# Pooled attention and a softplus feed-forward layer on one core: a chunk's steady attention regrouped into four interludes

## The chip, the cores and the metric

The program runs on one core of one Trainium2 chip. The metric is the device time of one execution in microseconds (us). TensorE (PE) multiplies matrices; its weight loads (PEld) run beside the multiplications. VectorE (DVE), ScalarE (ACT) and GpSimd (POOL) work on vectors, SyncE (SP) issues the transfers.

## The reference

```python
# q, k, v: (8, 8, 576, 64); pool = 8, Sp = 72
k_p = k.reshape(B, H, Sp, pool, D).mean(axis=3)
v_p = v.reshape(B, H, Sp, pool, D).mean(axis=3)
scores = scale * np.matmul(q, k_p.transpose(0, 1, 3, 2))
scores = scores - np.max(scores, axis=-1, keepdims=True)
attn = np.exp(scores)
attn = attn / (np.sum(attn, axis=-1, keepdims=True) + 1e-09)
attn_out = np.matmul(attn, v_p)
x = attn_out.transpose(0, 2, 1, 3).reshape(B * S, H * D)      # 4608 x 512
h = x @ w_in                                                  # 4608 x 2048
g = np.maximum(h, 0.0) + np.log1p(np.exp(-np.abs(h)))
return (g @ w_out).astype(np.float32)                         # 4608 x 512
```

## The kernel before

**Tiling.** The 4608 tokens are worked through in 18 chunks of 256 (`CT`), each of two tiles of 128 tokens. A chunk needs attention (its output x is 512 wide), then the first product (x with w_in), softplus, and the second product (with w_out). The feed-forward layer of a chunk runs in eight pairs u = 0 to 7, each of two blocks of 128 columns of w_in. Every number is kept as a rounded value and a rest, so that each product becomes three matmuls. In the steady part a pair is one block of 24 matmuls into `h` (line 562, 128x256 each, `pair1`) and one block of 21 matmuls into `m` (line 710, `pair2_fast`; seven products in place of eight). The blocks alternate on PE in a fixed order: h of pair u, then m of pair u - 1. After a block h, ACT makes g and its rounded part gh (lines 570, 584), DVE the sums `sf` (lines 621 to 624) and the rest gl (591), ACT rounds the sums (`so`, 635), DVE takes their rest (640); then the pair's block m may run.

**Attention one chunk ahead.** While chunk c runs through its eight pairs, the attention of chunk c + 1 is finished and that of c + 2 begun; its PE work stands as *interludes* between the blocks, sometimes inside a block h. Per tile these are: four transposes of q (`qT`, line 359), 32 small matmuls for the scores (`scores`, line 379, quarters of the array), four transposes of the normed probabilities (`PT`, 440) and two transposes of the probabilities of the last eight keys, in three copies (`last`, 452). Per chunk there is one interlude more, the values (`av_products`, 481 and 488). It has 20 matmuls, and 40 where the 256 tokens of the chunk belong to two batches of 576 tokens; below these are called split chunks (chunks 4, 6, 11, 13 and 15). In five chunks there are also four transposes of pooled keys (`kT`, line 232).

**Around them.** q goes from PSUM through ACT (366) to the scores; the scores through DVE (minimum 386, subtraction 393) into E; one exponential of ACT for both tiles (323, with a change of the activation table before and after it, placed behind the softplus of pair 2); then per tile DVE's sum (410), reciprocal (414, 415), `main` (419, keys 0 to 63) and `ends` (426, last eight keys), PE's transposes, ACT's copies (`PT_out` 447, `last_high` 459) and DVE's `last_low` (464); after the values ACT and DVE make x (495, 498).

**What sets the order.** `Order.run` (lines 52 to 100) is a list planner. Each `op(engine, cost, fn, after, slots, first)` has a planned cost, the operations it waits for, and slots (buffers of a kind) that it holds; the planner picks for each engine the operation with the longest remaining path plus `first` among those that could start by then or within `PAUSE` = 0.4 us. Each engine then executes its own list strictly in that order and waits where data are late. The kinds of slots (1259 to 1262) bound what may overlap: eight PSUM banks make two for the blocks h (`h`), four for accumulation (two of them kind `acc`), two for all of attention (`bank`); there are one `q`, one `pe`, two `qT`, one `E`, six `G`.

`steady_attention(c)` (1277) is called at pair 1 of chunk c - 1 and lists load, q and scores; `probabilities` (1309) lists the rest behind the exponential.

Of the kernel before, what the change touches and what calls it, by code (L numbers as in the profile page):

```python
# [30 lines left out]
class Order:  # L31
# [72 lines left out]
def pooled_attention_softplus_ffn(  # L104
# [9 lines left out]
    nc = tc.nc  # L114
# [220 lines left out]
    def load_q(c):  # L335
        new_q(c)
        for t in range(T):
            load_q_tile(c, t)
# [12 lines left out]
    class Tile:  # L351

        def __init__(self, c, t):
            self.c, self.t, self.first = c, t, c * CT + t * P
            self.ts = slice(t * P, (t + 1) * P)
# [106 lines left out]
        def last_low(self, ps):  # L462
            o = last_[self.c][R:2 * R, :, self.ts]
            nc.vector.tensor_tensor(
                out=o, in0=ps[R:2 * R, 0:2 * P].rearrange("p (a i) -> p a i", a=2),
                in1=o.bitcast(F32), op=ALU.subtract)

    def av_products(c, pss):

        pt, lt = pt_[c], last_[c]
        sp = [(b % 2, slice(lo - c * CT, hi - c * CT)) for lo, hi, b in spans(c * CT, (c + 1) * CT)]
        for g in range(2):
            for i, t in sp:
                for e in range(2):
                    for r, ps in enumerate(pss):
                        rows, n = slice(r * KM, (r + 1) * KM), 2 * g + e

                        nc.tensor.matmul(  # L481
                            out=ps[e * D:(e + 1) * D, g * CT + t.start:g * CT + t.stop],
                            lhsT=vs[i][rows, n], rhs=pt[rows, n, t],
                            start=g == 0 and t.start == 0, stop=False)
# [272 lines left out]
    def act(n):  # L757
        return 0.14 + 0.00094 * n
# [4 lines left out]
    def dve2(n):  # L763
        return 0.14 + 0.00106 * n
# [494 lines left out]
    kinds = {"h": other[:2], "acc": other[2:4], "bank": other[4:], "ld": LD, "q": "a", "pT": "a", "qT": Q, "lt_": "a",  # L1259
             "pe": "a", "mn": "ab", "sm": "ab", "E": "a", "kp": "a", "vp": "a", "S": "ab", "x": "b",  # L1260
             **{y.kind: {"a": "b", "b": "a"}[y.name] for y in last_g},
             "G": [f"G{i}" for i in range(4)] + O}
    ends = {e: max(o.end for o in todo.ops if o.engine == e) for e in (ACT, DVE, PE, SYNC)}
# [1 line left out]
    todo.begin = {e: max(0, t - ends[PE]) for e, t in ends.items()}  # L1265
    op = todo.op
    EXP, third = 2, {}
    HURRY, EARLY = 60, 100
    MM = 0.1195
    x_slot, x_done = {N1: taken[-1]}, {N1: []}  # L1270
    for x in (qT_done, score_done, av_done, k_ready, v_ready):
# [2 lines left out]

    parts_of = lambda n, k: [o for b in sorted({b for _, _, b in n}) for o in k.get(b, ())]

    def steady_attention(c):
        s_q, s_E, s_lt = Slot("q"), Slot("E"), Slot("lt_")
        tiles = [Tile(c, t) for t in range(T)]

        def load():
            load_q(c)
        o_q = op(SYNC, 3.0, load, qT_done.get(c - 1, ()), [s_q], lag=2.4)
        subs = []
        qT_done[c], score_done[c], av_done[c], x_done[c] = [], [], [], []
        for x in tiles:
            sp = spans(x.first, x.first + P)
            s, s_qT, s_mn = Slot("bank"), Slot("qT"), Slot("mn")
            o = op(PE, 0.45, lambda x=x, s=s: x.qT(bank(s, "qTp")), [o_q, *av_done.get(c - 1, ())],
                   [s_q, s], first=EARLY)  # L1290
            qT_done[c].append(o)
            o = op(ACT, act(512), lambda x=x, s=s, n=s_qT: x.qT_out(s.tile, n.name),
                   [o], [s, s_qT])
            last, ss = [], [Slot("bank"), Slot("bank")]
            p = op(PE, 0.7, lambda x=x, ss=ss: x.scores([bank(s, "sc") for s in ss]),
                   [o, *parts_of(sp, k_ready)], [s_qT, *ss], first=EARLY)
            score_done[c].append(p)
            for i, s in enumerate(ss):
                last = [op(DVE, 0.46, lambda x=x, i=i, s=s, n=s_mn: x.least(i, s.tile, n.name), [p, *last],
                           [s, s_mn])]  # L1300
# [5 lines left out]
                subs.append(op(DVE, 0.46, less, last, [s, s_mn, s_E]))  # L1306
        return lambda where: probabilities(c, tiles, s_E, s_lt, subs, where)

    def probabilities(c, tiles, s_E, s_lt, subs, where):

        s_pT, lows = Slot("pT"), []
        ex = op(ACT, 1.2 + TABLE, lambda: exponential(e_[c]), [*subs, where], [s_E])
        op(ACT, TABLE, lambda: None, [ex], first=5000)
        for x in tiles:
            s_sm, s_pm, s_pe = Slot("sm"), Slot("G"), Slot("pe")
            o = op(DVE, 0.76, lambda x=x, n=s_sm: x.sum(n.name), [ex], [s_E, s_sm])
            o = op(DVE, 0.38, x.reciprocal, [o], [s_sm])
            m = op(DVE, 0.7, lambda x=x, s=s_pm: x.main(s.name), [o], [s_E, s_sm, s_pm])
            e = op(DVE, 0.52, x.ends, [o], [s_E, s_sm, s_pe])
            s, r = Slot("bank"), Slot("bank")  # L1320
            o = op(PE, 0.45, lambda x=x, s=s: x.PT(bank(s, "ptp")), [m], [s, s_pm], first=EARLY)
            lows.append(op(ACT, act(512), lambda x=x, s=s: x.PT_out(s.tile), [o], [s, s_pT]))
            o = op(PE, 0.15, lambda x=x, r=r: x.last(bank(r, "ltp")), [e], [r, s_pe], first=EARLY)
            h = op(ACT, act(256), lambda x=x, r=r: x.last_high(r.tile), [o], [r, s_lt])
            lows.append(op(DVE, dve2(256), lambda x=x, r=r: x.last_low(r.tile), [h], [r, s_lt]))

        def values(after=()):
            sp = spans(c * CT, (c + 1) * CT)
            ss = [Slot("bank"), Slot("bank")]
            o = op(PE, 1.55 if len(sp) == 1 else 2.1,  # L1330
                   lambda: av_products(c, [bank(s, "avp") for s in ss]),
                   [*lows, *parts_of(sp, v_ready), *after], [*ss, s_lt, s_pT], first=EARLY)
            av_done[c].append(o)
            return o, ss
        o, ss = values()
        s_x = x_slot[c] = Slot("x")
        for r, s in enumerate(ss):
            o = op(ACT, act(512), lambda r=r, s=s: av_high(c, r, s.tile, s_x.name), [o], [s, s_x])
            x_done[c].append(op(DVE, dve2(512), lambda r=r, s=s: av_low(c, r, s.tile), [o], [s, s_x]))

    def first_products(c, u, before):
        fast = c >= NF
# [164 lines left out]
```

## Time and profile before

| what | value |
|---|---|
| median of 3 runs | 900.37 us (899.27 to 901.25) |
| span of the profiled execution | 899.4 us |
| PE busy in it | 884.2 us (98%) |
| PEld, DVE, ACT busy | 837.0, 649.1, 406.4 us |
| chain that ended last | 93% PE |
| read from and written to HBM | 167.25 and 22.54 MB |

Of the profiled execution the page gives the span, from the first instruction to the last; the runs are timed around the whole execution. The page's busy shares are averages over the span: up to about 187 us the weights are converted and the first three chunks are worked, up to 247 us chunk 3 runs with undivided second products, and from then to the end the steady pairs described above repeat.

In the rows below a line of the timeline merges neighbouring instructions of one kind: its first number is when the first of them started, the second how long they took together up to the modelled end of the last. Matmuls overlap, so what a block costs is read as the start of the next block less its own start.

### The profile page before, as it was taken

The page shows a single profiled execution, that of the slowest core. Times are in us where ns is not written, and L with a number is a line of the kernel's source. Part 1 is how long each engine was busy: PE and PEld are TensorE (multiplying, and loading weights), DVE is VectorE, ACT ScalarE, POOL GpSimd, SP SyncE. Part 2 cuts the span into 40 slices and gives each one's busy share as a digit, 9 for nine tenths or more (in the row PEclk, how much of TensorE's full clock was granted, in tenths as well). Part 3 has the DMA queues.
Part 4 walks back from the last instruction along what each step waited for, and adds up shares of the span by engine and source line. Part 5 has one row for each costly group of instructions (what it writes and reads, how often), then busy time and mean ns, then how long its engine had stood idle before and what let it go on. Part 6 is the DMA issues. An engine that isn't in the chain of part 4 may idle for free.

```text
span 899.4 us, 20521 instructions
## 1 busy us (share of the span) xinstructions
PE 884.2 (98%) x8308; PEld 837.0 (93%) x8308; DVE 649.1 (72%) x1601; ACT 406.4 (45%) x824; POOL 2.4 (0%) x19
## 2 busy tenths in 40 slices
PE   7999999999999999999999999999999999999997
PEld 3788989888999999999999999999999999999997
DVE  5989999888767778777667766777566565747454
ACT  5954343354353545444444435353545344434332
POOL 1000000000000000000000000000000000000000
PEclk9999999999999999999999999999999999999999
DMA  8974535455897777687658775677556565636472
GB/s 237 297 239 166 187 128 169 156 197 169 286 287 250 226 242 258 224 235 238 216 187 262 225 222 199 215 252 229 209 172 222 193 211 185 237 143 223 177 239 89
DMA packets 107085, 191.12 MB, mean 212 GB/s; under 512 B 46064, under 2 KB 60400, under 8 KB 106992
## 3 DMA queue, kind: packets, MB, share of 16 engines
q1 hardware_dynamic: 106992, 189.82, 64.9%
q8 instruction: 65, 1.06, 0.5%
q14 instruction: 28, 0.23, 0.1%
HBM read 167.25 MB, written 22.54 MB: 211 GB/s over the span
## 4 chain that ended last, share of the span: by engine, by line
PE 93%; DMA 3%; DVE 2%; SPq 1%; ACT 1%; issue 0%; DVEq 0%; ACTq 0%
PE h L562 37%; PE m L710 30%; PE acc L536 7%; PE h L514 7%; PE acc L603 3%; PE sc L379 2%; PE qTp L359 2%; PE avp L481 2%; PE ptp L440 1%; DMA wst<-in_moe_w_in_dram 1%; PE avp L488 1%; DMA w<-wi 1%; PE ltp L452 1%; DMA q<-in_q_dram 1%; DVE o L731 0%
## 5 line engine op out<-in xcount | busy, mean ns | idle before, releaser
L562 PE MATMUL h<-x,w 128*128 128x256 f32 x2880 | 354.4, 279 | 1.1 <-DVE x L498 0.8
L562 PEld LDWEIGHTS h<-x,w 128*128 128x128 f32 x2880 | 339.6, 188 | 2.6 <-PE acc L536 1.2
L570 ACT ACTIVATE g<-h 128x512 f32<-128x512 f32 x120 | 71.8, 598 | 277.6 <-PE h L562 277.5
L710 PE MATMUL m<-w,so 128*128 128x256 f32 x1344 | 172.4, 277 | 0.0
L710 PEld LDWEIGHTS m<-w,so 128*128 128x128 f32 x1344 | 162.3, 188 | 0.1
L710 PE MATMUL m<-w,gh 128*128 128x256 f32 x672 | 131.0, 284 | 0.0
L621 DVE TENSOR_TENSOR sf<-g 128x128 f32<-128x128 f32 x112 | 32.6, 291 | 134.2 <-ACT g L570 133.7
L710 PEld LDWEIGHTS m<-w,gh 128*128 128x128 f32 x672 | 101.6, 188 | 1.7
L635 ACT CAST so<-sf 128x512 fp32r<-128x512 f32 x112 | 69.7, 622 | 57.4 <-DVE sf L624 57.1
L640 DVE TENSOR_TENSOR so<-sf,so 128x512 fp32r<-128x512 f32 x112 | 77.3, 690 | 22.4 <-ACT so L635 22.4
L710 PE MATMUL m<-w,gl 128*128 128x256 f32 x336 | 93.4, 278 | 0.0
L514 PEld LDWEIGHTS h<-x,w 128*128 128x128 f32 x576 | 71.8, 188 | 3.3 <-DVE w L849 0.4
L514 PE MATMUL h<-x,w 128*128 128x256 f32 x576 | 73.3, 279 | 0.0
L591 DVE TENSOR_TENSOR gl<-g,gh 128x384 fp32r<-128x384 f32 (+1 forms) x120 | 67.3, 561 | 2.2 <-PE ltp L452 1.7
L710 PEld LDWEIGHTS m<-w,gl 128*128 128x128 f32 x336 | 63.1, 188 | 0.0
L519 ACT ACTIVATE g<-h 128x256 fp32r<-128x256 f32 x96 | 32.2, 383 | 65.9 <-PE h L514 46.5
L536 PE MATMUL acc<-w,g 128*128 128x512 f32 x192 | 61.0, 398 | 0.0
L584 ACT ACTIVATE gh<-h 128x384 fp32r<-128x384 f32 (+1 forms) x120 | 59.3, 494 | 0.0
L731 DVE TENSOR_TENSOR o<-o,m 128x256 f32<-128x256 f32 x98 | 39.7, 418 | 3.3 <-ACT o L723 0.4
L536 PE MATMUL acc<-w,gl 128*128 128x512 f32 x96 | 38.0, 396 | 1.0 <-DVE gl L525 1.0
L536 PEld LDWEIGHTS acc<-w,g 128*128 128x128 f32 x192 | 33.3, 188 | 5.4
L624 DVE TENSOR_TENSOR sf<-g,sf 128x128 f32<-128x128 f32 x112 | 32.7, 292 | 3.9
(170 smaller groups left out, 979.7 us busy)
## 6 DMA issues: line engine op xcount, KB each, us to landing
w<-wi SPq DMA_DIRECT2D x224, 512.0 KB
out_dram<-o SPq DMA_DIRECT2D x36, 256.0 KB
q<-in_q_dram SPq DMA_DIRECT2D x32, 256.0 KB
wst<-in_moe_w_in_dram SPq DMA_DIRECT2D x32, 256.0 KB
wst<-in_moe_w_out_dram SPq DMA_DIRECT2D x16, 512.0 KB
wi<-w SPq DMA_DIRECT2D x16, 512.0 KB
kst<-in_k_dram SPq DMA_DIRECT2D x24, 288.0 KB
vst<-in_v_dram SPq DMA_DIRECT2D x24, 256.0 KB
```

The lines of the kernel that those rows point to most:

```text
L514: nc.tensor.matmul(out=ps[:, 0:CT], lhsT=row(w, kc), rhs=x[:, kc], start=first and kc == j == 0, stop=last and kc == KC - 1 and j == 2)
L536: nc.tensor.matmul(out=accs[c][t], lhsT=a[:, ts], rhs=w, start=f == 0 and j == 0, stop=f == FC - 1 and j == 2)
L562: nc.tensor.matmul(out=ps[:, k * CT:(k + 1) * CT], lhsT=row(w, kc), rhs=x_[c][i][:, kc], start=first and n == 0, stop=last and n == len(or ...
L570: nc.scalar.activation(out=g, in_=x.rearrange("p (b i) -> p b i", i=P), func=AF.Softplus)
L584: nc.scalar.activation(out=gh, in_=quarters(c, x.rearrange("p (b i) -> p b i", i=P)), func=AF.Softplus)
L591: nc.vector.tensor_tensor(out=gl, in0=quarters(c, g), in1=gh.bitcast(F32), op=ALU.subtract)
L621: tt(out=sf[:, 2], in0=g[:, 0], in1=g[:, 2], op=ALU.add)
L624: tt(out=sf[:, 3], in0=g[:, 3], in1=sf[:, 1], op=ALU.subtract)
L635: nc.scalar.copy(out=so[:, 0], in_=ss[c, u])
L640: nc.vector.tensor_tensor(out=so[:, 1], in0=sf, in1=so[:, 0].bitcast(F32), op=ALU.subtract)
L710: nc.tensor.matmul(out=ms[c][n], lhsT=x, rhs=y, start=u == 0 and j == 0 and n in (1, 6, 5, 4), stop=u == FP - 1 and j == 2 and n in (2, 7, ...
L731: nc.vector.tensor_tensor(out=o, in0=in0, in1=m[n], op=how)
```

## The change

The steady part's attention (chunk 4 and later) is listed anew; what is computed stays the same.

- PE: the two tiles' `PT` and the four transposes of the last keys become one operation of 12 transposes, which waits for `main` of both tiles and for `ends`. The values and the first four q transposes of the *next* chunk become one operation, which also waits for the load of that q. The scores of tile 0 and the q transposes of tile 1 become one operation. The scores of tile 1 stay alone.
- Banks: the last keys (of both tiles together, in one bank), and both q transposes, use a bank of kind `h`; before they used kind `bank`.
- DVE: one sum, one addition and one reciprocal for both tiles; `ends` in three instructions for both tiles in place of four; `last_low` once in place of twice. ACT: `last_high` once in place of twice. `pe` (now for both tiles) takes a buffer of kind `qT`.
- SP: the load of the next chunk's q is listed with the probabilities, still behind the q transposes of the chunk before.
- Planner: minima, subtractions, `last_high` and `last_low` get `first=FRONT` (20).

```diff
-             "pe": "a", "mn": "ab", "sm": "ab", "E": "a", ...
+             "pe": "a", "mn": "ab", "sm": "a", "E": "a", ...
-    HURRY, EARLY = 60, 100
+    HURRY, EARLY, FRONT = 60, 100, 20
+    class Chunk:
...
+        def sum(self, tag):
+            sm = self.sm = small.tile([P, T * H], F32, tag="sm" + tag, name="sm")
+            nc.vector.tensor_reduce(out=sm, in_=self.E(), axis=AX.X, op=ALU.add)
...
+        def ends(self, tag):
+            self.pe = one.tile([P, 2 * T, 3, R], F32, tag=tag, name="pe")
+            for n in range(3):
+                nc.vector.tensor_tensor(out=self.pe[:, :, n]..., in0=self.E()[:, :, KM:SP]..., op=ALU.mult)
+        def PT(self, pss, psl):
+            for t, ps in enumerate(pss):
+                for n in range(HP):
+                    nc.tensor.transpose(out=ps[:, n * P:(n + 1) * P], in_=self.pm[t][:, 2 * n:2 * n + 2]..., identity=ident)
+            for t in range(T):
+                for a in range(2):
+                    nc.tensor.transpose(out=psl[0:3 * R, a * CT + t * P:...], in_=self.pe[:, 2 * t + a]..., identity=ident)
...
     def steady_attention(c):
+        if c not in firsts:
+            first_q(c)
...
+        for t, x in enumerate(tiles_[c]):
+            r = Slot("h") if t == 0 else None
+            def scores(t=t, x=x, ss=ss, r=r):
+                x.scores([bank(s, "sc") for s in ss])
+                if t == 0:
+                    tiles_[c][1].qT(bank(r, "qTp"))
+            p = op(PE, 1.15 if t == 0 else 0.7, scores, [o, *parts_of(..., k_ready)],
+                   [s_qT, *ss, *([r, s_q] if t == 0 else [])], first=EARLY)
...
+    def probabilities(c, s_E, s_lt, subs, where):
...
+        o = op(DVE, 1.65, lambda: x.sum(s_sm.name), [ex], [s_E, s_sm])
+        e = [op(DVE, 0.7, lambda t=t: x.main(t, s_pm[t].name), [o], [s_E, s_sm, s_pm[t]]) for t in range(T)]
+        e.append(op(DVE, 0.8, lambda: x.ends(s_pe.name), [o], [s_E, s_sm, s_pe]))
+        bs = [Slot("bank"), Slot("bank"), Slot("h")]
+        o = op(PE, 1.3, lambda: x.PT([bank(s, "ptp") for s in bs[:2]], bank(bs[2], "ltp")), e,
+               [*bs, *s_pm, s_pe], first=EARLY)
+        h = op(ACT, act(512), lambda: x.last_high(bs[2].tile), [o], [bs[2], s_lt], first=FRONT)
+        lows = [op(DVE, dve2(512), lambda: x.last_low(bs[2].tile), [h], [bs[2], s_lt], first=FRONT)]
+        lows += [op(ACT, act(512), lambda t=t: x.PT_out(t, bs[t].tile), [o], [bs[t], s_pT]) for t in range(T)]
...
+        if more:
+            load_queries(c + 1)
+            r, (s_q, o_q) = Slot("h"), q_loads[c + 1]
+        def values():
+            av_products(c, [bank(s, "avp") for s in ss])
+            if more:
+                tiles_[c + 1][0].qT(bank(r, "qTp"))
+        o = op(PE, (1.55 if len(sp) == 1 else 2.1) + 0.45 * more, values,
+               [*lows, *parts_of(sp, v_ready), o_q], [*ss, s_lt, s_pT, *([r, s_q] if more else [])], first=EARLY)
```

## Rows read from the trace of the kernel before

**Rows 1.** The page: the span, and the busy time of each engine (share of the span, instructions).

```profile
span 899.4 us, 20521 instructions
PE 884.2 (98%) x8308; PEld 837.0 (93%) x8308; DVE 649.1 (72%) x1601; ACT 406.4 (45%) x824; POOL 2.4 (0%) x19
```

**Rows 2.** The page's groups of instructions: line, engine, operation, tiles, shapes, count; busy us, mean ns of one; idle time of the engine before them and what ended it.

```profile
L635 ACT CAST so<-sf 128x512 fp32r<-128x512 f32 x112 | 69.7, 622 | 57.4 <-DVE sf L624 57.1
L640 DVE TENSOR_TENSOR so<-sf,so 128x512 fp32r<-128x512 f32 x112 | 77.3, 690 | 22.4 <-ACT so L635 22.4
```

**Rows 3.** Timeline of PE, two stretches without attention: from 527.72 us and from 670.22 us: a block h, the first line of the block m behind it, the next block h; and the next interlude after 670.22 us.

```profile
527.72 2.88 PE L562 MATMUL h<-x,w 128*128 128x256 f32 x24
530.44 0.39 PE L710 MATMUL m<-w,gh 128*128 128x256 f32 x2
...
532.82 2.88 PE L562 MATMUL h<-x,w 128*128 128x256 f32 x24
...
670.22 2.99 PE L562 MATMUL h<-x,w 128*128 128x256 f32 x24
673.05 0.40 PE L710 MATMUL m<-w,gh 128*128 128x256 f32 x2
...
675.52 2.99 PE L562 MATMUL h<-x,w 128*128 128x256 f32 x24
...
691.43 1.04 PE L440 MATMUL ptp<-ident,pm 128*128 128x128 f32 x8
```

**Rows 4.** Timeline of PE, all interludes of one chunk, 501 to 526 us; of each block h or m only its first line, and of the six transposes from 504.50 us only the first two.

```profile
501.09 0.60 PE L440 MATMUL ptp<-ident,pm 128*128 128x128 f32 x4
501.44 3.22 PE L562 MATMUL h<-x,w 128*128 128x256 f32 x24
504.50 0.38 PE L452 MATMUL ltp<-ident,pe 128*96 128x128 f32 x2
...
505.08 0.49 PE L710 MATMUL m<-w,gh 128*128 128x256 f32 x2
...
507.64 0.38 PE L452 MATMUL ltp<-ident,pe 128*96 128x128 f32 x2
507.78 2.99 PE L562 MATMUL h<-x,w 128*128 128x256 f32 x24
510.70 1.09 PE L481 MATMUL avp<-pT,vs 64*64 64x256 f32 x16
...
512.30 0.40 PE L710 MATMUL m<-w,gh 128*128 128x256 f32 x2
...
514.70 1.04 PE L359 MATMUL qTp<-ident,q 128*128 128x128 f32 x8
515.49 2.98 PE L562 MATMUL h<-x,w 128*128 128x256 f32 x24
518.39 0.73 PE L379 MATMUL sc<-kT,qT 64*64 64x72 f32 x32
519.05 0.50 PE L710 MATMUL m<-w,gh 128*128 128x256 f32 x2
...
521.63 2.99 PE L562 MATMUL h<-x,w 128*128 128x256 f32 x24
524.55 0.73 PE L379 MATMUL sc<-kT,qT 64*64 64x72 f32 x32
525.21 0.50 PE L710 MATMUL m<-w,gh 128*128 128x256 f32 x2
```

**Rows 5.** Timeline of PE: the first and the last of the 24 scores interludes between 249 and 892 us, with what stands before and behind it, and between them the values of a split chunk with a line of the block m behind it (the 12 matmuls `m<-w,so`) and the block h that follows its eight q transposes. The first scores stand inside a block h, between two runs of 12 matmuls.

```profile
284.11 1.62 PE L562 MATMUL h<-x,w 128*128 128x256 f32 x12
285.65 0.73 PE L379 MATMUL sc<-kT,qT 64*64 64x72 f32 x32
286.31 1.68 PE L562 MATMUL h<-x,w 128*128 128x256 f32 x12
...
747.85 1.11 PE L481 MATMUL avp<-pT,vs 64*64 64x192 f32 x32
...
750.59 1.58 PE L710 MATMUL m<-w,so 128*128 128x256 f32 x12
...
753.15 2.98 PE L562 MATMUL h<-x,w 128*128 128x256 f32 x24
...
806.18 2.99 PE L562 MATMUL h<-x,w 128*128 128x256 f32 x24
809.10 0.73 PE L379 MATMUL sc<-kT,qT 64*64 64x72 f32 x32
...
810.57 1.52 PE L710 MATMUL m<-w,so 128*128 128x256 f32 x12
```

**Rows 6.** Timeline of PE: transposes of pooled keys (72 rows) directly ahead of four transposes of P (that line is left out), the block m behind both, and further on a block h behind four transposes alone.

```profile
545.74 0.42 PE L232 MATMUL kT<-ident,kp 72*128 72x72 f32 x4
...
546.60 0.48 PE L710 MATMUL m<-w,gh 128*128 128x256 f32 x2
...
549.52 2.98 PE L562 MATMUL h<-x,w 128*128 128x256 f32 x24
```

**Rows 7.** Timeline of PE, the one wait inside a block h of the steady part.

```profile
408.23 2.15 PE L562 MATMUL h<-x,w 128*128 128x256 f32 x16 [0.36 <-DMA w<-wi]
```

**Rows 8.** The windows view of the steady part (us, then busy us of PE, PEld, DVE, ACT, POOL with instructions, granted clock, DMA share, GB/s).

```profile
249.00:892.00 643.00, 642.53 (x6332) 629.78 (x6331) 433.80 (x1182) 284.71 (x505) 0.00 (x0) 1.00 0.67 218
```

More of the change, by code (lines that the diff above doesn't have):

```diff
@@ L1259, in pooled_attention_softplus_ffn @@
     kinds = {"h": other[:2], "acc": other[2:4], "bank": other[4:], "ld": LD, "q": "a", "pT": "a", "qT": Q, "lt_": "a",
-             "pe": "a", "mn": "ab", "sm": "ab", "E": "a", "kp": "a", "vp": "a", "S": "ab", "x": "b",
+             "pe": "a", "mn": "ab", "sm": "a", "E": "a", "kp": "a", "vp": "a", "S": "ab", "x": "b",
              **{y.kind: {"a": "b", "b": "a"}[y.name] for y in last_g},
@@ L1275, in pooled_attention_softplus_ffn @@
     parts_of = lambda n, k: [o for b in sorted({b for _, _, b in n}) for o in k.get(b, ())]
-    def steady_attention(c):
[L1278 to L1296, printed above, removed]
+    tiles_, q_loads = {}, {}
@@ new lines, in load_queries, with q_out, first_q @@
+    def load_queries(c):
+        s_q = Slot("q")
+        tiles_[c] = [Tile(c, t) for t in range(T)]
+        q_loads[c] = s_q, op(SYNC, 3.0, lambda: load_q(c), qT_done.get(c - 1, ()), [s_q], lag=2.4)
+        for x in (qT_done, score_done, av_done, x_done):
+            x[c] = []
+    def q_out(c, t, o, s):
+        s_qT = Slot("qT")
+        o = op(ACT, act(512), lambda: tiles_[c][t].qT_out(s.tile, s_qT.name), [o], [s, s_qT])
+        return o, s_qT
+    firsts = {}
+    def first_q(c):
+        load_queries(c)
+        s_q, o = q_loads[c]
+        s = Slot("bank")
+        o = op(PE, 0.45, lambda: tiles_[c][0].qT(bank(s, "qTp")), [o], [s_q, s], first=EARLY)
+        firsts[c] = q_out(c, 0, o, s)
@@ new lines, in steady_attention @@
+    def steady_attention(c):
+        if c not in firsts:
+            first_q(c)
+        s_E, s_lt, s_q = Slot("E"), Slot("lt_"), q_loads[c][0]
+        subs, q = [], firsts[c]
+        for t, x in enumerate(tiles_[c]):
+            o, s_qT = q
+            s_mn, ss = Slot("mn"), [Slot("bank"), Slot("bank")]
+            r = Slot("h") if t == 0 else None
+            def scores(t=t, x=x, ss=ss, r=r):
+                x.scores([bank(s, "sc") for s in ss])
+                if t == 0:
+                    tiles_[c][1].qT(bank(r, "qTp"))
+            p = op(PE, 1.15 if t == 0 else 0.7, scores,
+                   [o, *parts_of(spans(x.first, x.first + P), k_ready)],
+                   [s_qT, *ss, *([r, s_q] if t == 0 else [])], first=EARLY)
@@ L1297, in steady_attention @@
             score_done[c].append(p)
+            if t == 0:
+                qT_done[c].append(p)
+                q = q_out(c, 1, p, r)
+            last = []
             for i, s in enumerate(ss):
                 last = [op(DVE, 0.46, lambda x=x, i=i, s=s, n=s_mn: x.least(i, s.tile, n.name), [p, *last],
-                           [s, s_mn])]
+                           [s, s_mn], first=FRONT)]
                 def less(x=x, i=i, s=s):
@@ L1305, in less @@
                     x.less(i, s.tile)
[L1306 to L1311, printed above, removed]
+                subs.append(op(DVE, 0.46, less, last, [s, s_mn, s_E], first=FRONT))
+        return lambda where: probabilities(c, s_E, s_lt, subs, where)
+    def probabilities(c, s_E, s_lt, subs, where):
+        x = Chunk(c)
@@ L1312, in probabilities @@
         ex = op(ACT, 1.2 + TABLE, lambda: exponential(e_[c]), [*subs, where], [s_E])
         op(ACT, TABLE, lambda: None, [ex], first=5000)
[L1314 to L1335, printed above, removed]
-        s_x = x_slot[c] = Slot("x")
-        for r, s in enumerate(ss):
-            o = op(ACT, act(512), lambda r=r, s=s: av_high(c, r, s.tile, s_x.name), [o], [s, s_x])
-            x_done[c].append(op(DVE, dve2(512), lambda r=r, s=s: av_low(c, r, s.tile), [o], [s, s_x]))
+        s_pT, s_sm, s_pe = Slot("pT"), Slot("sm"), Slot("qT")
@@ new lines, in probabilities @@
+        s_pm = [Slot("G") for _ in range(T)]
+        o = op(DVE, 1.65, lambda: x.sum(s_sm.name), [ex], [s_E, s_sm])
+        e = [op(DVE, 0.7, lambda t=t: x.main(t, s_pm[t].name), [o], [s_E, s_sm, s_pm[t]])
+             for t in range(T)]
+        e.append(op(DVE, 0.8, lambda: x.ends(s_pe.name), [o], [s_E, s_sm, s_pe]))
+        bs = [Slot("bank"), Slot("bank"), Slot("h")]
+        o = op(PE, 1.3, lambda: x.PT([bank(s, "ptp") for s in bs[:2]], bank(bs[2], "ltp")), e,
+               [*bs, *s_pm, s_pe], first=EARLY)
@@ new lines, in probabilities @@
+        h = op(ACT, act(512), lambda: x.last_high(bs[2].tile), [o], [bs[2], s_lt], first=FRONT)
+        lows = [op(DVE, dve2(512), lambda: x.last_low(bs[2].tile), [h], [bs[2], s_lt], first=FRONT)]
+        lows += [op(ACT, act(512), lambda t=t: x.PT_out(t, bs[t].tile), [o], [bs[t], s_pT])
+                 for t in range(T)]
+        sp = spans(c * CT, (c + 1) * CT)
+        ss, more = [Slot("bank"), Slot("bank")], c + 1 < NCH
+        r, s_q, o_q = None, None, None
+        if more:
+            load_queries(c + 1)
+            r, (s_q, o_q) = Slot("h"), q_loads[c + 1]
@@ new lines, in values @@
+        def values():
[3 more added lines that the diff above has]
+        o = op(PE, (1.55 if len(sp) == 1 else 2.1) + 0.45 * more, values,
+               [*lows, *parts_of(sp, v_ready), o_q], [*ss, s_lt, s_pT, *([r, s_q] if more else [])],
+               first=EARLY)
+        av_done[c].append(o)
+        s_x = x_slot[c] = Slot("x")
+        for i, s in enumerate(ss):
+            h = op(ACT, act(512), lambda i=i, s=s: av_high(c, i, s.tile, s_x.name), [o], [s, s_x])
+            x_done[c].append(op(DVE, dve2(512), lambda i=i, s=s: av_low(c, i, s.tile), [h], [s, s_x]))
@@ L1341, in first_products @@
+        if more:
+            firsts[c + 1] = q_out(c + 1, 0, o, r)
     def first_products(c, u, before):
```

35 lines of the change are left out of this document (added).

## The prediction

> **What bounds the kernel now.** Read the page first: PE is busy 98% of the span, DVE 72%, ACT 45% [rows 1]. Then the windows view: in the steady part, 249 to 892 us, PE is busy 642.53 of 643.00 us at a granted clock of 1.00 [rows 8]. So nothing that DVE, ACT or a queue saves is worth time there; only what PE executes, and how fast, counts.
>
> Then the timeline of PE, because "busy" hides two paces. From 527.72 us a block h lasts 2.72 us and a block m 2.38, a pair 5.10; from 670.22 us the same matmuls, on the same engine at the same clock, take 2.83, 2.47 and 5.30 [rows 3]. That is 0.20 us a pair, over 45 matmuls 4.4 ns each. I call them the fast and the slow pace. No engine is waited for in either, and a pace lasts until the next interlude: the slow one of 670.22 holds for four pairs, to the next transposes at 691.43. Which pace follows an interlude is thus worth more than it looks.
>
> Third, what an interlude costs beside its own work [rows 4]. Four transposes take 0.35 us from their start to the next block, eight 0.79, and the block behind is 0.10 longer (549.52: 2.98 against 2.88 as listed) [rows 3, 4, 6]. So four cost 0.45 and eight 0.89: two separate fours are 0.90. Transposes have almost no price per interlude. The scores do: 0.66 of their own, 0.09 on the block before (521.63 to 524.55 is 2.92 against 2.83) and 0.11 on the one behind (519.05 to 521.63 is 2.58 against 2.47), and both scores interludes stay.
>
> **The change part by part.**
>
> *The transposes of P and of the last keys.* Before, in this chunk, three interludes: 0.35 + 0.58 + 0.14 and three times 0.10, 1.37 us [rows 4]. After, twelve in one: 0.79 for eight, four more at (0.79 - 0.35) / 4 = 0.11, one 0.10: 1.33. Gain 0.04 a chunk.
>
> *Values with the next q, scores with the other q.* The eight q transposes (0.89 with their edge) become two fours behind other work. No row shows transposes behind values or scores. The best end is that the 0.10 edge is paid once: -0.10 a merge. The worst is the nearest row of unlike neighbours: pooled keys and P together take 0.86 up to the block m [rows 6], which leaves 0.51 for the keys where four full transposes take 0.35, so +0.16. The values end in full-height matmuls, as a block does (only 0.02 on the block behind: 512.30 to 514.70 is 2.40 against 2.38), and scores must hand over to full-height work anyway; so I take what eight against four and four shows, -0.01 each. Over 14 chunks the three merges give -(0.04 + 0.02) x 14 = -0.8 us, with ends at -2.8 and +4.5 for the two unlike ones.
>
> *Where the interludes stand.* Before, the chain is drawn out by the single `pe`, by two banks and by seven interludes: 26.63 us from the first transposes to the first undisturbed block, four pairs [rows 3, 4]. After, the four can stand at four successive block ends, since the work between them is short: ACT's copy and DVE's subtraction of 512 columns are 0.62 and 0.69 us [rows 2], against blocks of 2.4 to 2.8. Three blocks then lie between interludes, and about six of a chunk's eight pairs run undisturbed behind the second scores, where it was four.
>
> *The pace.* In the chunk shown the slow blocks are those from 501.44, 505.08, 519.05 and 521.63: 90 matmuls, 0.40 us. Over 13 chunks 5.2 us, and the long slow stretch from 670.22 adds four pairs, 0.8. After, if all three blocks between interludes are slow, 24 + 21 + 24 matmuls cost 0.30 a chunk, 3.9 us in all; and undisturbed blocks are fast if the second scores leave the fast pace. Gain 1.3 + 0.8 = 2.1.
>
> *DVE, ACT, SP.* Fewer and larger instructions, hidden behind PE's unbroken stream: nothing. If that cover goes, it is by order, not by amount: one sum for both tiles holds DVE longer in one go (a rival below prices such a delay). The load of the next q is issued earlier, past transfers of `w<-wi` on SP's one queue. A late `w<-wi` has cost PE 0.36 us once [rows 7]; it may vanish (-0.4) or come in every chunk (14 x 0.36 = +5.0). I take it as gone, since the q load leaves the place just ahead of a chunk's first blocks. Values now also wait for that load, with every block queued behind them on PE; issued a whole chunk ahead, it lands in time: nothing.
>
> Sum: -0.8 - 2.1 - 0.4 = -3.3 us. Against the span of the profiled execution, 899.4, that is 896.1; the median of the runs, 900.37, lies 0.97 above that span, so I forecast **897.1 us**.
>
> **The rivals.** The pace is the open point, because it seems to be turned by the interludes. All 24 scores interludes of the steady part turn it over, the first from fast to slow (1.62 for 12 matmuls before, 1.68 behind), the last from slow to fast (a listed block of 2.99 before, then 1.52 for 12) [rows 5]. Eight transposes mostly leave it (514.70: fast before and behind); four turn it (501.09: the block behind is slow) [rows 3, 4]. Values of an unsplit chunk always leave the fast pace (512.30 to 514.70), those of a split one the slow pace (1.58 at 750.59) [rows 4, 5].
>
> *Split chunks stay slow.* By these turns, after unsplit values the four q transposes give slow, scores fast, q slow, scores fast, as I forecast; after split values everything is reversed and six pairs run slow. Four such chunks in the steady part: 4 x 6 x 0.20 = +4.8, 901.9 us. Against it: the turns are no law; the split chunk shown came back to the fast pace at its eight q transposes (the block at 753.15, listed with 2.98, is a fast one with the edge of 0.10) [rows 5].
>
> *Unsplit chunks stay slow (the slower side).* If values with q leave the pace that their last matmuls have, the second scores leave the slow one. It decides at the block behind the second scores, at 1.2 us a chunk. Nine chunks: +10.8, 907.9 us; with the split ones too 912.7. For it: no row shows q behind values or scores. Against it: the stretch from 670.22, behind a split chunk, is the only one of the steady part before that ran slow behind second scores.
>
> *A bank is late.* Three interludes a chunk now take one of the two banks of the blocks h. If the twelve transposes stand directly behind a block h, the next block h needs their bank after one block m, 2.38 us [rows 3]. `last_high` 0.62, `last_low` 0.69 and one `so` subtraction ahead of it 0.69 make 2.0 [rows 2]: it fits. A further DVE operation of 0.69 ahead of it makes PE wait 0.31: 13 x 0.31 = +4.0, 901.1 us. Against it: the planner counts banks and may put them behind a block m, where the bank is wanted much later. The Trainium skill, in "Perfetto Trace Analysis", section "Optimizing Tensor Performance", asks that independent groups of matmuls rotate through different PSUM banks so that one's evacuation overlaps the next; by that rule sharing the two banks of h speaks against this change, and the time would be the 901.1 or more just named. No row of before shows a wait for a bank.
>
> *Edges are saved.* Both unlike merges pay one edge less: -2.8, 894.3 us.
>
> *The clock falls.* Twelve transposes in a row for 1.33 us would count if PE's clock fell from its level of 2.4 to 1.2 GHz behind them; one block h would then take some 2.7 us more, 13 x 2.7 = +35. The granted clock is 1.00 over the whole steady part, the eight in a row at 514.70 included [rows 4, 8]. The Trainium skill, in "TensorE: Matmul & The Clock Gate", section "Part 4: PE-mode transpose", says that transposes do not count as PE work for the clock gate as matmuls do; the trace shows no fall, so it keeps a small chance.
>
> **How the numbers follow.** Forecast 0.42 (0.37 of it faster, 0.05 same); split chunks slow 0.22 (0.13 same, 0.09 slower); unsplit slow 0.17; late bank 0.10 (half same, half slower); edges saved 0.06; clock 0.03. A measurement of this kernel can tell 0.2%, 1.8 us, from no change. So faster 0.43, same 0.23, slower 0.34. The range goes from 893.5, just below the saved edges, to 908.0, just above nine slow chunks; it leaves out thirteen slow chunks, two DVE operations ahead of the bank, and the clock. The two merges' worst end (+4.5) and late weights (+5.0) lie inside it.
>
> **What would show it.** In the timeline of PE: 12 transposes at 1.2 to 1.3 us, four interludes at successive block ends, about six undisturbed pairs a chunk. Right: these pairs at 5.10 us in nearly all chunks. Wrong: 5.30 behind the second scores (split or unsplit chunks tell the rivals apart), PE idle time ahead of a block h ended by ACT or DVE (the bank), `w<-wi` waits, or blocks more than 0.11 longer behind merged scores.

## The result, and the profile after

The changed kernel takes **904.64 us** (median; 903.99 to 907.46) where the kernel before takes 900.37 (898.48 to 901.25). The ratio is 1.0063, 95% interval 1.0044 to 1.0082: slower, by 0.6%. The forecast was 897.1, so the sign is wrong; the range held the time.

The page of the changed kernel: the span, and the busy time of each engine, as in [rows 1].

```profile
span 902.5 us, 20508 instructions
PE 889.2 (99%) x8308; PEld 843.2 (93%) x8308; DVE 644.3 (71%) x1531; ACT 402.5 (45%) x810; POOL 2.4 (0%) x19
```

PE is busy 5.0 us more with the same 8308 matmuls; DVE has 70 instructions fewer and ACT 14, and both are less busy. The cost lies where PE works without a pause. The windows view of the steady part (us, then busy us of PE, PEld, DVE, ACT, POOL, granted clock, DMA share, GB/s) has PE busy all the time, so the 0.36 us that [rows 7] show are gone and no new wait has come. The stretch of four undisturbed pairs from 570.38 us lasts 21.20 us, 5.30 a pair, at the granted clock of the steady part of before [rows 8], 1.00.

```profile
570.38:591.58 21.20, 21.20 (x182) 21.20 (x181) 15.84 (x41) 9.74 (x15) 0.00 (x0) 1.00 0.81 249
249.00:894.00 645.00, 645.00 (x6312) 633.06 (x6311) 427.65 (x1114) 280.37 (x490) 0.00 (x0) 1.00 0.66 217
```

The timeline of PE, one chunk (split values): of each block its first line only, as in [rows 3] and [rows 4].

```profile
548.78 2.89 PE L620 MATMUL h<-x,w 128*128 128x256 f32 x24
551.51 1.03 PE L501 MATMUL ptp<-ident,pm 128*128 128x128 f32 x8
552.38 0.60 PE L507 MATMUL ltp<-ident,pe 128*96 128x128 f32 x4
552.74 0.48 PE L768 MATMUL m<-w,gh 128*128 128x256 f32 x2
...
555.29 2.99 PE L620 MATMUL h<-x,w 128*128 128x256 f32 x24
558.21 1.11 PE L539 MATMUL avp<-pT,vs 64*64 64x64 f32 x32
559.25 1.14 PE L546 MATMUL avp<-lt__7414,vlo 96*128 96x64 f32 x8
560.23 0.60 PE L359 MATMUL qTp<-ident,q 128*128 128x128 f32 x4
560.59 0.49 PE L768 MATMUL m<-w,gh 128*128 128x256 f32 x2
...
563.16 0.73 PE L379 MATMUL sc<-kT,qT 64*64 64x72 f32 x32
563.82 0.66 PE L359 MATMUL qTp<-ident,q 128*128 128x128 f32 x4
564.23 2.98 PE L620 MATMUL h<-x,w 128*128 128x256 f32 x24
567.15 0.73 PE L379 MATMUL sc<-kT,qT 64*64 64x72 f32 x32
567.81 0.50 PE L768 MATMUL m<-w,gh 128*128 128x256 f32 x2
...
570.38 2.99 PE L620 MATMUL h<-x,w 128*128 128x256 f32 x24
...
575.68 2.99 PE L620 MATMUL h<-x,w 128*128 128x256 f32 x24
...
580.98 2.99 PE L620 MATMUL h<-x,w 128*128 128x256 f32 x24
...
586.28 2.99 PE L620 MATMUL h<-x,w 128*128 128x256 f32 x24
...
591.58 2.99 PE L620 MATMUL h<-x,w 128*128 128x256 f32 x24
...
596.88 2.99 PE L620 MATMUL h<-x,w 128*128 128x256 f32 x24
599.71 1.04 PE L501 MATMUL ptp<-ident,pm 128*128 128x128 f32 x8
```

Read it in this order. The four interludes start at 551.51, 558.21, 563.16 and 567.15: two blocks lie between the first two, one between the others. The twelve transposes take 1.23 us (551.51 to 552.74). The values with the four q transposes behind them take 2.38 (558.21 to 560.59), the first scores with theirs 1.07 (563.16 to 564.23). The second scores, 0.66, close the group after 16.3 us, where the seven interludes of [rows 4] took 24.1 (501.09 to 525.21). Then come five undisturbed pairs, from 570.38, 575.68, 580.98, 586.28 and 591.58 to 596.88. Each is 5.30 us, the slow pace of [rows 3]. The block of 564.23, between the two scores, is a fast one: 2.98 as listed, as the block at 753.15 in [rows 5].

This chunk is one of three in which the interludes stand so close (45 matmuls, then 21, then 24 between them). In the other nine, of the 12 from 250 us to the end, a whole pair lies between each two: the chunk from 361.02 takes 21.0 us to the block behind its second scores, and five pairs follow undisturbed where this one has six. No chunk has all four at successive block ends.

So the second scores come in fast and leave slow. They do this in 11 of the 12 chunks. The twelfth shows what the others could have been; its second scores last longer than 0.66 us, and the pairs behind them are 5.10 (337.57, 342.67, 347.77):

```profile
334.19 0.95 PE L379 MATMUL sc<-kT,qT 64*64 64x72 f32 x32
...
337.57 2.88 PE L620 MATMUL h<-x,w 128*128 128x256 f32 x24
...
342.67 2.88 PE L620 MATMUL h<-x,w 128*128 128x256 f32 x24
...
347.77 2.88 PE L620 MATMUL h<-x,w 128*128 128x256 f32 x24
```

### The profile page after: what moved, and what is told of

It is laid out like the page before. It is cut to its first block, busy times and chain, and to the rows that moved or that the text cites. A ratio compares the mean times of both kernels' runs of the same rounds, so it can differ in the third digit from the quotient of the medians.

```text
span 902.5 us, 20508 instructions
## 1 busy us (share of the span) xinstructions
PE 889.2 (99%) x8308; PEld 843.2 (93%) x8308; DVE 644.3 (71%) x1531; ACT 402.5 (45%) x810; POOL 2.4 (0%) x19
## 4 chain that ended last, share of the span: by engine, by line
PE 93%; DMA 3%; DVE 2%; ACT 1%; issue 0%; SPq 0%; DVEq 0%; ACTq 0%
PE h L620 37%; PE m L768 30%; PE h L572 6%; PE acc L594 6%; PE sc L379 3%; PE acc L661 3%; PE qTp L359 2%; PE avp L539 2%; PE avp L546 1%; PE ptp L501 1%; DMA vst<-in_v_dram 1%; DMA q<-in_q_dram 1%; PE ltp L507 1%; DMA kvst<-in_v_dram 1%; PE vps L1023 1%; PE kps L1006 1%
## 5 line engine op out<-in xcount | busy, mean ns | idle before, releaser
L768 PE MATMUL m<-w,so 128*128 128x256 f32 x1344 | 174.5, 279 | 0.0
```

Source lines behind the costliest of these rows:

```text
L768: nc.tensor.matmul(out=ms[c][n], lhsT=x, rhs=y, start=u == 0 and j == 0 and n in (1, 6, 5, 4), stop=u == FP - 1 and j == 2 and n in (2, 7, ...
```

## The experiments

All are built from the changed kernel unless another base is named; "the kernel before" was run beside each. Counts in the text below are of the 12 chunks from 250 us to the end (those quoted in the expectations include earlier chunks). A constant transpose is one of the identity into a part of the scores' bank that nothing reads.

**More work behind the second scores: one, two, three and four constant transposes** (`range(1)` to `range(4)`).

```diff
                 x.scores([bank(s, "sc") for s in ss])
                 if t == 0:
                     tiles_[c][1].qT(bank(r, "qTp"))
+                else:
+                    for _ in range(1):
+                        nc.tensor.transpose(out=bank(ss[1], "sc")[:, HP * SP:HP * SP + P],
+                                            in_=ident, identity=ident)
```

> The same with one more transpose. Added work 14 x 0.11 = 1.5 us. Theory: near 904.6 + 1.5 - 10.6 = 895.5 if one is enough to turn the pace, near 906.1 if not. Rival: 906.1 whatever the pace does.

> The same with two more transposes. Added work 14 x 0.22 = 3.1 us. Theory: two possible times, near 904.6 + 3.1 - 10.6 = 897.1 if two are enough to turn the pace, near 907.7 if not, and the pace of the undisturbed blocks (5.10 or 5.30) says which. Rival: 907.7 whatever the pace does.

> The changed kernel with three constant transposes behind each second scores. One left the fast pace 16 times of 16, two 12 of 16, four none. Theory A, a phase that drifts with the number: mostly slow, about 4 fast of 16, slow blocks some 10 us, 905 to 908. Theory B, odd numbers leave fast and even ones less so: fast, 897 to 899.

> The changed kernel with four more transposes of a constant behind the second scores of each chunk (14 chunks), in unused columns of a scores bank; the order on every engine is otherwise the same. Theory (the pace behind the second scores is what was lost): in the changed kernel every scores group followed by four transposes, 13 of 13, leaves the fast pace, so the undisturbed blocks behind go from 5.30 to 5.10 us a pair; 11 slow stretches of together 48 pairs and 11 blocks m give back 48 x 0.20 + 11 x 0.09 = 10.6 us, the added work costs 14 x 0.44 = 6.2: 4.4 us faster than the changed kernel's 904.6, near 900.2. Rival (the loss sits in the longer merged interludes or in waits, the pace only goes along): 6.2 slower, near 910.8.

| transposes added to each second scores | time, us | ratio to before (95%) | pace behind them |
|---|---|---|---|
| 0 (the changed kernel) | 904.64 | 1.0063 (1.0044 to 1.0082) | slow in 11 of 12 |
| 1 | 895.85 | 0.9956 (0.9936 to 0.9976) | fast in 12 of 12 |
| 2 | 897.47 | 0.9978 (0.9962 to 0.9993) | fast in 12 of 12 |
| 3 | 908.31 | 1.0111 (1.0080 to 1.0142) | slow in 12 of 12 |
| 4 | 909.52 | 1.0112 (1.0095 to 1.0130) | slow in 12 of 12 |

One transpose that computes nothing makes the changed kernel 8.8 us faster than without it, and faster than the kernel before. Timeline of PE with one added, one chunk, of each block its first line:

```profile
562.86 0.73 PE L379 MATMUL sc<-kT,qT 64*64 64x72 f32 x32
563.52 0.33 PE L1374 MATMUL sc<-ident 128*128 128x128 f32 x1
563.61 0.48 PE L768 MATMUL m<-w,gh 128*128 128x256 f32 x2
...
566.09 2.88 PE L620 MATMUL h<-x,w 128*128 128x256 f32 x24
...
571.18 2.88 PE L620 MATMUL h<-x,w 128*128 128x256 f32 x24
...
576.28 2.88 PE L620 MATMUL h<-x,w 128*128 128x256 f32 x24
...
581.38 2.88 PE L620 MATMUL h<-x,w 128*128 128x256 f32 x24
...
586.49 3.05 PE L620 MATMUL h<-x,w 128*128 128x256 f32 x24
...
591.84 2.99 PE L620 MATMUL h<-x,w 128*128 128x256 f32 x24
```

Pairs of 5.10 (566.09, 571.18, 576.28, 581.38, 586.49) stand where the changed kernel had 5.30. The windows view of four of them (columns as above) gives 20.40 us for the work that took 21.20, with the clock at 1.00 in both:

```profile
566.09:586.49 20.40, 20.40 (x183) 20.40 (x182) 15.72 (x41) 9.66 (x15) 0.00 (x0) 1.00 0.79 242
```

The block of 586.49 is another sign: it is listed with 3.05, has one gap of 210 ns between two matmuls at 587.39, and the pace is slow behind it (591.84 is 5.35 later), with no interlude anywhere near. With three added, the same place looks like this:

```profile
569.65 0.73 PE L379 MATMUL sc<-kT,qT 64*64 64x72 f32 x32
570.31 0.55 PE L1374 MATMUL sc<-ident 128*128 128x128 f32 x3
570.61 0.49 PE L768 MATMUL m<-w,gh 128*128 128x256 f32 x2
...
573.17 2.99 PE L620 MATMUL h<-x,w 128*128 128x256 f32 x24
...
578.48 2.99 PE L620 MATMUL h<-x,w 128*128 128x256 f32 x24
```

570.61 stands 0.30 behind 570.31, so three transposes cost 0.1 each, and the pairs are back at 5.30 (573.17 to 578.48). The sign of the time thus follows the pace, not the amount of work. The expectation of four, that scores with four transposes always leave the fast pace, fell: with the four q transposes they do so 12 times of 12, with four constant ones never.

**One constant transpose ahead of the second scores.** The same line, but before `x.scores` (for `t == 1`).

> The changed kernel with one constant transpose ahead of each second scores (not behind them, where one made it 895.85). Theory A, the pace behind an interlude is set at its hand-over, by what PE executes last: the scores still hand over, so the undisturbed pairs stay at 5.30 us, and the transposes add 14 x 0.1 = 1.4 us and an entry each: 906 to 907. Theory B, any added operation shifts the phase and one more turns it, wherever it stands: 5.10 us, and 896 as with the one behind.

897.31 us, ratio 0.9977 (0.9953 to 1.0001), fast behind the second scores in 12 of 12. It comes near the 896 of theory B; but B in its words, any added operation, does not hold either, since three or four transposes behind the scores leave the pace slow. Theory A, that the last work of an interlude decides, fell: in both kernels the scores hand over, and the block behind starts alike (0.46 from 564.00 to the second `m<-w,gh` line here, 0.45 from 567.81 in the changed kernel).

```profile
563.14 0.27 PE L1370 MATMUL sc<-ident 128*128 128x128 f32 x1
563.34 0.73 PE L379 MATMUL sc<-kT,qT 64*64 64x72 f32 x32
564.00 0.50 PE L768 MATMUL m<-w,gh 128*128 128x256 f32 x2
...
566.50 2.88 PE L620 MATMUL h<-x,w 128*128 128x256 f32 x24
...
571.60 2.88 PE L620 MATMUL h<-x,w 128*128 128x256 f32 x24
```

**One narrow matmul behind the second scores.**

```diff
+                else:
+                    nc.tensor.matmul(out=bank(ss[1], "sc")[:, HP * SP:HP * SP + 16], lhsT=ident,
+                                     rhs=ident[:, 0:16], start=True, stop=True)
```

> The changed kernel with one matmul of 16 columns of a constant behind the second scores instead of a transpose of 128: at most 0.05 us each, 0.7 in all. Theory: near 904.6 + 0.5 - 10.6 = 894.5 if so little already turns the pace, 905.1 if not; which of the two is open. Rival: 905.1 whatever the pace does.

908.18 us, 1.0111 (1.0091 to 1.0131), slow in 12 of 12. The size was misjudged: it runs as two matmuls and the interlude grows by 0.244 us (0.905 for 0.661), more than two transposes. Again added work leaves the second scores at the slow pace, and the kernel got slower.

**The q transposes ahead of the first scores, not behind them** (`tiles_[c][1].qT(...)` moved above `x.scores(...)`).

> The changed kernel with the four q transposes ahead of the first scores in their common interlude, not behind; no work added, the same order otherwise. Theory: the pace ahead of the second scores then follows from scores that stand last, which turn the pace that they meet; behind unsplit values with q it is mostly slow, four transposes make it fast, scores slow again, so the second scores leave the fast pace in most unsplit chunks: between 895 and 901. Rival (order within an interlude does not matter): 904.6, within 1.

907.72 us, 1.0085 (1.0066 to 1.0105): a miss. I had expected that another order would turn the pace. The merged interlude leaves the fast pace in either order (12 of 12), and the second scores left the slow one in 11. One wait of 3.7 us for DVE ahead of the pooled keys (289.03) comes on top in the profiled execution. Behind this idle time the granted clock fell to its lower level, 1.2 GHz: it reads 0.50 from 291 to 293 us, the second scores there took 1.17 us for 0.66, and matmuls followed each other at 213 ns.

**The second q as an operation of its own**, which the planner puts directly behind the values and the first q.

```diff
-                if t == 0:
-                    tiles_[c][1].qT(bank(r, "qTp"))
-            p = op(PE, 1.15 if t == 0 else 0.7, scores,
+            p = op(PE, 0.7, scores,
...
+                d = op(PE, 0.45, lambda r=r: tiles_[c][1].qT(bank(r, "qTp")),
+                       [q_loads[c][1], *av_done.get(c - 1, ())], [r, s_q], first=EARLY)
```

> One part of the change undone: the q transposes of the second tile are an interlude of their own again (behind the values, where the planner puts them), the scores of the first tile stand alone; all else as changed. Theory (pace): scores alone turn the pace, so with eight transposes or four and four ahead of them the second scores meet the slow pace and leave the fast one, as in the kernel before; the slow matmuls fall from 12.9 to about 3.5 us, one edge more costs 14 x 0.05 = 0.7: near 896. Rival (the loss is in the twelve transposes and the values with q): no more than 1 us from 904.6.

902.77 us, 1.0039 (1.0025 to 1.0053): a miss again. Bare scores turned the pace over 24 times of 24, as in the kernel before, but the values with eight transposes left it fast 5 times and slow 7, so the pairs behind two turns were fast or slow as it fell.

**The same with one constant transpose behind the second scores.** The expectation below says ahead; in the kernel that ran, and in its trace, the transpose stands behind.

> The second q as an operation of its own (902.77 alone; slow blocks 11.0 us), with one constant transpose ahead of its second scores. Theory A, the hand-over decides: the scores still hand over, the pace behind them is what it was, 904 to 905. Theory B, any added operation turns it: slow blocks fall to about 3 us, 895 to 896.

899.03 us, 0.9984 (0.9970 to 0.9998). Timeline of PE, the second scores of one chunk:

```profile
567.38 0.73 PE L379 MATMUL sc<-kT,qT 64*64 64x72 f32 x32
568.04 0.33 PE L1371 MATMUL sc<-ident 128*128 128x128 f32 x1
```

The slow pace cost 3.9 us, near the 3 of theory B. But the scores do not hand over here, so theory A's 904 to 905 was worked out for another kernel, and this run cannot tell the two theories apart; the run with one transpose ahead of the changed kernel's second scores does. What it adds: the second scores with one transpose behind them left the fast pace in 12 of 12, whether they came in fast (8) or slow (4). The time did not come down to 895, as there were new waits. The waits view of PE (line, what is waited for, us, times, longest):

```profile
PE h L620 <- DMA w<-wi: 2.6, 3, 0.9
PE m L768 <- DVE gl L649: 0.5, 1, 0.5
```

Some 3 us. A faster PE asks for its weights sooner; that this made them late is likely, but not shown.

**Only the twelve transposes**: the changed kernel's P and last keys, with the q transposes, scores and values of the kernel before.

> One part of the change alone: the twelve transposes of P in one interlude with their DVE and ACT work for both tiles, and the last keys in a bank of the blocks h; q, scores and values as in the kernel before (eight q transposes together, both scores alone). Theory: edges 13 x 0.05 = 0.7 us less, fast pace behind the second scores as before, fewer blocks between interludes: near 898. Rival (the twelve transposes lose the time, by their bank or their length): slower than 900.4, towards 904.6.

901.04 us, 1.0010 (0.9995 to 1.0026): no change. The pace is as before (second scores slow to fast in 12 of 12). Timeline of PE around one chunk's transposes and second scores, first lines only. The first line carries the one longer wait; its bracket says for how long and for what:

```profile
501.21 2.10 PE L620 MATMUL h<-x,w 128*128 128x256 f32 x16 [0.82 <-DMA w<-wi]
503.14 1.04 PE L501 MATMUL ptp<-ident,pm 128*128 128x128 f32 x8
504.01 0.60 PE L507 MATMUL ltp<-ident,pe 128*96 128x128 f32 x4
...
506.93 2.99 PE L620 MATMUL h<-x,w 128*128 128x256 f32 x24
...
523.71 0.73 PE L379 MATMUL sc<-kT,qT 64*64 64x72 f32 x32
...
526.88 2.88 PE L620 MATMUL h<-x,w 128*128 128x256 f32 x24
...
531.98 2.88 PE L620 MATMUL h<-x,w 128*128 128x256 f32 x24
```

The pairs behind the second scores are 5.10 (526.88 to 531.98), and no block that follows the twelve transposes waits for their bank: 504.01 to 506.93 runs through. Over the steady part PE is charged with 0.8 us for `w<-wi`, the bracket above, and 0.2 for `qT`.

**P and last keys per tile as before, the rest changed.**

> The changed kernel with P and the last keys per tile, in three interludes as before; q stays merged with the values and the first scores. Pace theory: second scores follow scores with q, which leave the fast pace, so they leave the slow one; fewer pairs run undisturbed because the interludes are drawn out, about four for six: slow blocks 10 us for 12.9, three edges for one: 903 to 905. Rival, the twelve transposes in a row are what costs the time: 899 or less.

907.11 us, 1.0077 (1.0059 to 1.0094). The second scores left the slow pace in 12 of 12, as the pace theory said; the time is 2 us above its range, since the slow blocks cost 14.8 us and not 10. The rival, that the twelve transposes in a row are what costs the time, fell.

**The kernel before with one constant transpose behind the second scores.**

> The kernel before with one more transpose of a constant behind the second scores of each chunk, as in the run with one more on the changed kernel, the order otherwise as before. Theory: if the transpose turns the pace there, some 12 stretches of 4 pairs run slow, 12 x 4 x 0.20 = +9.6, and 14 x 0.09 for the work: near 911; if it leaves it fast, near 901.6; the timeline must show 5.30 or 5.10 accordingly. Rival (the pace has no part in it): 901.6 in either case.

899.28 us, 0.9994 (0.9980 to 1.0007): no change. The second scores came in slow and left fast in 11 of 12, with the transpose as without it. The twelfth came in fast: without the transpose it left slow (666.99, the stretch of [rows 3] from 670.22), with it fast (664.22). So with one transpose behind them scores leave the fast pace whatever they come in with: 36 times of 36 over this run, the changed kernel with one behind, and the second q alone with one behind (21 from fast, 15 from slow).

## Why the prediction was wrong

**The account.** PE never stops, so its time from 250 us to the end is a sum of four parts, read over the whole timeline of PE: all `h` and `m` matmuls at 113.3 ns from start to start (the fast pace), the excess of those that follow each other at 115.5 to 126 ns (the slow pace, 117.7 in its run), waits (gaps that stand out from others of their kind), and what is left: the interludes with their edges. The sum against before is of the last three parts. It leaves out that the kernels have not done the same number of matmuls by 250 us: the changed kernel is 10 ahead there, 1.1 us, and the most is 29. Each part in us, of the profiled execution:

| kernel | matmuls at the slow pace | their excess | waits | interludes, edges | sum against before | ratio of the times |
|---|---|---|---|---|---|---|
| before | 1391 of 4961 | 6.32 | 0.52 | 75.38 | | 1 |
| changed | 2885 of 4951 | 12.88 | 0.22 | 73.46 | +4.3 | 1.0063 |
| + 1 behind | 699 | 3.11 | 0.41 | 74.45 | -4.3 | 0.9956 |
| + 2 behind | 660 | 2.93 | 3.32 | 75.80 | -0.2 | 0.9978 |
| + 3 behind | 3066 | 13.71 | 0 | 76.88 | +8.4 | 1.0111 |
| + 4 behind | 3046 | 13.58 | 0 | 78.12 | +9.5 | 1.0112 |
| + 1 ahead | 668 | 2.97 | 0.39 | 75.01 | -3.8 | 0.9977 |
| narrow matmul | 3029 | 13.49 | 0 | 76.14 | +7.4 | 1.0111 |
| q ahead of scores | 2895 | 12.95 | 4.67 | 74.72 | +10.1 | 1.0085 |
| second q alone | 2472 | 11.04 | 0 | 74.09 | +2.9 | 1.0039 |
| the same + 1 behind | 879 | 3.93 | 4.05 | 75.79 | +1.6 | 0.9984 |
| P per tile | 3298 | 14.76 | 1.31 | 74.21 | +8.1 | 1.0077 |
| only the P merge | 1258 | 5.67 | 1.83 | 74.31 | -0.4 | 1.0010 |
| before + 1 | 1014 | 4.58 | 0 | 75.89 | -1.7 | 0.9994 |

For the changed kernel: +6.6 slow pace, -0.3 waits, -1.9 interludes and edges, in all +4.3; less the 1.1 of the 10 matmuls this is what the spans differ by, 3.1. The medians lie 4.3 apart; the ratio says 5.7 (4.0 to 7.4). Over all rows the sum and the ratio differ by 1.5 us in the mean and 3.0 at most: the sum leaves out the time before 250 us, and its waits are those of one execution.

Where the slow matmuls stand settles it. Behind the second scores, up to the next chunk's first transposes, the excess went from 1.1 us before to 10.5 (forecast 0.8 to 0); between the interludes it went from 5.2 to 2.4 (forecast 5.2 to 3.9).

**The step that failed** is the pace: "undisturbed blocks are fast if the second scores leave the fast pace". The forecast took -2.1 for it; it measured +6.6. The half of the rule that says that bare scores turn the pace over held: 24 of 24 in the kernel before, with the second q alone and with only the P merge; 11 of 12 here. What failed is the other half, "four transposes turn it", carried over from transposes that stood alone to q transposes behind scores. Scores with four q transposes leave the fast pace whatever they came in with (12 of 12 in the changed kernel: 6 from fast, 6 from slow). The second scores thus always start from the fast pace, and their one turn ends in the slow one. Before, two bare scores made two turns. Scores with transposes behind them, then, need not turn the pace that they meet: with four q transposes, or with one constant one, they left the fast pace from either.

A second step was off without deciding the sign: only three of 12 chunks came near "three blocks between interludes, about six undisturbed pairs"; nine have six blocks between and about five pairs behind.

**The rivals.** "Unsplit chunks stay slow, the split ones too" is what happened, by another way than it was priced: not the values but the first scores set it. It gave 912.7: an excess of 3.9 + 13 x 1.2 = 19.5 us, of which 12.88 came. The pooled keys' transposes turn part of the undisturbed pairs back to fast, one chunk stayed fast (337.57), and the blocks between the interludes were not all slow (564.23). "Split chunks stay slow" alone is ruled out: split and unsplit chunks end alike. "A bank is late" did not come: PE waits for no bank in the steady part, and the twelve transposes at the end of a block h left the next one on time. The change goes against the rule of the Trainium skill named there ("Perfetto Trace Analysis", section "Optimizing Tensor Performance"), that independent groups of matmuls rotate through different PSUM banks, and in this case that cost nothing: PE was busy 645.00 of 645.00 us. "Edges are saved" was right in sign (see the merges), and too small to decide. "The clock falls" did not come: 1.00 over 249 to 894 us, the level of 2.4 GHz.

**The merges.** Forecast -0.8 in all. The -1.9 of the account is not theirs alone. Take for each interlude the time from the start of the last `h` or `m` matmul ahead of it to the start of the second one behind, less 226.7 ns for two steps at the fast pace. P and the last keys fall from 1.35 to 1.33 us a chunk, -0.3 over 13 chunks (0.02 each against the 0.04 taken). Values, q and scores fall from 4.32 to 4.26 in unsplit chunks and from 4.75 to 4.68 in split ones, -0.7 over 12 chunks, some -0.03 a merge where -0.01 was taken. Both together are -1.0, within the ends given. Another -0.6 comes from the pooled keys, which the forecast left out: directly ahead of P, as in three chunks before, they cost 0.51 us, and alone, as now in all five, 0.31.

**The weights' wait**, -0.4 forecast, went (-0.5 in the account). It came back in faster variants, in other places: 0.2 us with one transpose behind, 0.5 with two, 2.6 with the second q alone and one behind, and 0.8 with only the P merge.

**What stays open.** What makes one interlude turn the pace and another not. It is neither the number of transposes alone (1 and 2 fast, 3 and 4 slow, but four q transposes behind the first scores fast), nor what stands last (one transpose ahead does the same as one behind), nor the clock (1.00 in both paces) or a wait (none in either); the DMA share was 0.81 in the slow pairs from 570.38 us and 0.79 in the fast ones with one transpose added. The weight loads do not show it: in both paces one starts 2 to 5 ns after a matmul does. A gap of 97 ns beyond the 113 inside an undisturbed stretch turned it as well (587.39 us with one transpose added), and so did the second scores of 334.19 in the changed kernel, 0.22 us longer than the others. The other way, a gap of 156 ns in a slow stretch with the narrow matmul added (595.50 us) was followed by the fast pace. A phase between two things on PE, set at a hand-over and then kept, would look like this; which two, no view here shows, and no run tested it.

## What to carry to other kernels

When an engine is busy all the time, read the start-to-start time of its equal instructions before and after, not its busy share: 4% in the pace of the bulk outweighed everything that seven interludes cut to four could save. Don't forecast such a pace by a rule from other surroundings; sort every transition of the trace by what came in, what ran and what came out, and price the change at both paces. Once a pace is seen to depend on a hand-over, trying one or two small shifts is cheap: here one idle transpose per chunk took the change from 0.6% slower to 0.4% faster than before.

## What the runs showed of the hardware that was not expected

- The same 128x256 matmuls follow each other at 113.3 or at 117.7 ns for tens of microseconds, at a granted clock of 1.00 in both, and keep it until something disturbs the stream.
- Work can make a kernel faster: 12 transposes of 0.1 us in the stretch from 250 us took 9.8 us of slow pace away (12.88 to 3.11).
- Scores alone turned the pace over (24 of 24 in the kernel before); scores with four q transposes behind them left the fast pace from either, 96 times of 96 over the eight kernels that have them, and scores with one constant transpose behind 36 of 36.
- An idle time of 3.69 us on PE was followed by a granted clock of 0.50 for some 3 us (q ahead of scores, 289 to 293 us).
- Transposes that follow each other have almost no price beyond 0.11 us each: twelve take 1.23 us (551.51 to 552.74).
- The 16-column matmul was recorded as two matmuls and added 0.244 us, more than two transposes of 128 columns (0.193, from 0.661 to 0.854).
